# A planner's durations set anew, and TensorE's order of the same units searched again

## The chip, the cores and the metric

The kernel runs on one core of a Trainium2 chip, with its five engines: TensorE (PE), which multiplies matrices into PSUM; VectorE (DVE) and ScalarE (ACT), which read PSUM and write SBUF; GpSimd (POOL), which computes in SBUF and issues DMAs; and SyncE (SP), which issues DMAs. Each engine works through its own queue in the order written. The metric is the time of one execution on the device, in microseconds (us).

## The reference: what is computed

Talking-heads attention, and then a feed-forward layer with a squared ReLU. There are 8 batches, 12 heads, 448 positions, 64 columns in a head; the layer goes from 768 to 2048 and back.

```
scores = einsum('bhij,hg->bgij', q k^T / 8, w_pre)
attn   = softmax(scores)
attn   = einsum('bhij,hg->bgij', attn, w_post)
x      = attn v,  heads side by side: 3584 x 768
out    = relu(x w_in)^2 w_out
```

w_pre and w_post mix the twelve heads, the first before the softmax and the second behind it.

## The kernel before

The kernel is a set of *tasks*, each a short piece of work of one engine, and a *planner* (`_Plan`) that puts them in order when the program is built. All of it is decided then; on the chip each engine runs its list and waits on semaphores.

The tasks of one batch follow the data. "tr" units (L718) transpose q and k on PE; "tev" copies bring them to SBUF as `qkt`. "qk" units (L864) form scores for a tile of up to 128 rows, two heads at a time; twelve "sev" copies put the tile into `stage` (L478 on ACT, L479 on DVE). "rel" transfers, issued by SP (L910), lay the scores of 10 rows and 12 heads on 120 partitions of one slot of `dring`, which has 16 slots: the relayout. Then a "pre" unit (L933) mixes heads with `wk1` for two such slots, two "exp" tasks on ACT (L950) form the exponentials and their sums in `pring`, "rec" on DVE takes reciprocals, and "fold" and "tail" on POOL (L971, L986) multiply them into the weights `wk2s` and into `ptail`. A "post" unit (L1016, L1031) mixes heads again, and two "a2ev" copies bring the result to `a2t` (L478, L479). When half of a batch's rows are there, three "av" units (L1097) multiply by v and "xtev" copies give `xt`. The feed-forward layer has "h" units (F1; L1148 in batches 0 and 1, L1176 in the others), "relu" and "sq" tasks (L1204 or L1205, L1214), and "o" units (F2; L1293, the last two tiles L1242), each half of a unit pair of 16 matmuls; copies "oev" and transfers "odma" by POOL bring the output away. Batch 0 takes a shorter way for its first 22 slots: "dir" units (L815) with q scaled by the weights (products "sc", L793). Its weights `w_in_sb` and `w_out_sb` are loaded meanwhile. Before the first data "warm" matmuls (L591) run on a constant, and later in some gaps of the first 60 us; how many is worked out from the gap that the planner expects.

PE's units belong to ten streams (tr, qk, pre, post, av, dir, two of F1, two of F2), and the order within a stream is fixed. Which stream comes next is a digit of the string `ORDER`, one digit per unit: 948 of them. A program outside of the kernel searched for that string with the planner's costs. The planner (`run`, L306) takes PE's units in that order and places every other task by itself: of the tasks whose inputs it takes to be ready, the one that can start first; a copy or ReLU marked `FLEX` goes to ACT or DVE, whichever it expects to finish sooner. So the order on ACT, DVE, POOL and SP follows from the costs too.

```
streams = [[] for _ in range(10)]
s_T, s_QK, s_pre, s_post, s_AV, s_dir = streams[:6]
s_F1, s_F2 = streams[6:8], streams[8:]
...
per_engine, _ = plan.run(ORDER)
```

Each task has a cost per engine, `(held, lat)`: how long it occupies the engine, and after how long its result can be used. PE's costs are in `c_pe` and `unit`, the general ones of copies in `c_ev`. A change of the array's mode between units (row halves, quarters, column halves, full) costs `MODE_SWITCH`. Transfers are modelled as two kinds, "move" (relayouts) and "load" (the rest): a start (`DMA_START`, and up to `DMA_AHEAD` behind loads already on the way), work that slows while both kinds move (`dma_next`), and an end (`DMA_END`). `FETCH` (`fetch_wait`) prices PE's fetching of instructions, in blocks of 256. PSUM has eight banks; a unit takes the one or two that come free first, and waits for the copies that read them.

Of the kernel before, what the change touches and what calls it, by code (L numbers as in the profile page):

```python
# [10 lines left out]
PE = "pe"  # L11
# [7 lines left out]
MODE_SWITCH = 106.0  # L19
ACT_BIAS = 14.5  # L20
BLOCK = 256
FETCH = (110e3, 6000.0, 4600.0, 1400.0)
DMA_START = {"move": 1420.0, "load": 1350.0}
DMA_AHEAD = 3900.0
DMA_SLOW = {"move": 1.0, "load": 1.04}
DMA_END = {"move": 3700.0, "load": 2300.0}
INF = float("inf")
ORDER = (
    "0011055055105510551555511155555553115550013555555553135002555555335555335531002555112551"
    "1233332412423432266311771316622237673313676331677222444312767612267731367331671216767322"  # L30
    "2679339339221922833831020182244430026721810038111811181318322667133762227667331673337226"
    "2244433276113177300226761116722833833382128002672117667020367223833831181118122442293391"
    "3193119223932193139224422443393163116117200272263163723733632167022076211673372200833811"
    "1822289111933391139222244383183318113822244442236116317137116226373020273621363723722006"
    "2116733720209331913191192228183318331822224439319111933392224444222838316316338113822711"
    "7200263363722176313637212762002673317242020913191119133922244181338221831381383228224441"
    "3813633836702207622267117611633733762126733720018381228382200919111911393224422913931931"
    "3922283811383138322444422267161373611366222673173713736223673217392219812938338398222444"
    "22833873833867667672227676367678338444867676767676677679989998889899"
# [60 lines left out]
class _Plan:  # L100
# [97 lines left out]
    def dma_push(self, t, start):  # L198
# [3 lines left out]
        if kind == "move" and at < 30e3:  # L202
            at += 600.0
        elif kind == "move" and not self.moving["move"]:
            behind = sum(x[1] for x in self.moving["load"] if x[0] <= at)
            at += min(DMA_AHEAD, max(0.0, behind - max(0.0, at - self.moved)))
        self.moving[kind].append([at, work, packet, t])

    def dma_next(self, go=False):
# [7 lines left out]
        while True:  # L217
# [6 lines left out]
            if all(on):  # L224
                rate = (0.22, 0.52)
                if b[2] <= 200.0:
                    rate = (47.8 / (54.0 + b[2]), 0.72)
# [10 lines left out]
        if go:  # L238
            self.moved = now
            for i, y in enumerate((a, b)):  # L240
                if y is not None:
# [4 lines left out]
                        + (1800.0 if t.dma[0] == "load" and 20e3 < now < 45e3 else 0.0))  # L246
# [98 lines left out]
def bass_talking_heads_attention__then__ffn_squared_relu_kernel(  # L345
# [45 lines left out]
    with ExitStack() as es:  # L391
# [68 lines left out]
        def c_pe(t):  # L460
            return {PE: (t, t + 190.0)}
# [9 lines left out]
        def unit(s, name, fn, deps, ns, mode, group, mms):  # L471
            t = add(name, PE, fn, deps, c_pe(ns), 0, mode, group, 2 * mms)
# [156 lines left out]
        def load_v(b, u, h0, deps, after, prio):  # L629
            def fn(eng, en):  # L630
# [7 lines left out]
                            dma=("load", 870.0, 60.0))  # L638
# [63 lines left out]
        def emit_T(b):  # L702
            pb = b % 2
            for a in range(3):
                g = _Group(2)
                trs = []
                for i, src in enumerate((qraw, kraw)):
# [5 lines left out]
                    def fn_tr(eng, en, a=a, g=g, i=i, src=src, o0=o0):  # L713
                        r_ = None
                        for t in range(NT):
                            o = o0 + (POS[t] if i else t) * PJ
                            for u, c in QUADS:
# [9 lines left out]
                                7 * 32.0 + 18.0, "quad", g, 4 * NT)  # L727
# [20 lines left out]
                for u in range(2):  # L748
                    p = 3 * u + a

                    def fn_ev(eng, en, u=u, p=p, g=g):
# [3 lines left out]
                               {ACT: (820.0, 970.0), DVE: (545.0, 625.0)}, b * 1000.0 - 700)  # L755
# [91 lines left out]
        def emit_QK(b, T):  # L847
# [8 lines left out]
            for p in ((0, 3, 1, 4, 2, 5) if n == 0 else range(0, NP, IT // w)):  # L856
                g = _Group(2)

                def fn_qk(eng, en, p=p, g=g):
                    r_ = None  # L860
                    for x, y in QUADS:
                        if y * w < IT:
# [13 lines left out]
                            205.0 if quad else 190.0, "quad" if quad else "row", g,  # L876
                            4 if quad else 2)
                t_qk.after += old
                for x, y in QUADS:
# [3 lines left out]
                    def fn_sev(eng, en, x=x, y=y, p=p, g=g):  # L883
# [4 lines left out]
                                c_ev(S), b * 1000.0 + 20 + 10 * T)  # L888
# [14 lines left out]
        def emit_rel(b, c, n, r0, d0, nv):  # L903
# [4 lines left out]
            def fn(eng, en):  # L908
# [5 lines left out]
                         {SP: (850.0 if b == 0 else 1050.0, 0.0)}, g * 1.0, sem, 16,  # L914
# [10 lines left out]
        def emit_pre(g0):  # L925
# [3 lines left out]
            def fn_pre(eng, en):  # L929
                r_ = None  # L930
                for x, y in QUADS:
                    if x < len(gs):
# [7 lines left out]
                         205.0, "quad", gr, 2 * len(gs))  # L940
# [4 lines left out]
        def after_pre(g, t_pre, gr, x):  # L945
# [3 lines left out]
            def fn_exp(eng, en):  # L949
# [4 lines left out]
                        {ACT: (520.0, 645.0)}, b * 1000.0 - 900 + c)  # L954
# [8 lines left out]
            def fn_rec(eng, en):  # L963
# [3 lines left out]
                        {DVE: (82.0, 160.0)}, b * 1000.0 - 900 + c)  # L967

            def fn_fold(eng, en):
# [7 lines left out]
                         {POOL: (330.0, 370.0), DVE: (200.0, 280.0)},  # L977
# [7 lines left out]
            def fn_tail(eng, en):  # L985
# [6 lines left out]
                         {POOL: (340.0, 380.0), DVE: (200.0, 280.0)},  # L992
# [6 lines left out]
        def emit_post(g0):  # L999
# [10 lines left out]
            def fn_post(eng, en):  # L1010
# [12 lines left out]
                for x in range(2):  # L1023
# [5 lines left out]
                    else:  # L1029
# [8 lines left out]
                          nr * 28.0 + 2.0, "row", gr, 2 * nr)  # L1038
# [3 lines left out]
            for x in range(2):  # L1042
                def fn_a2(eng, en, x=x):
# [8 lines left out]
                           {ACT: c_ev(nr * PR * 1.16)[ACT], DVE: c_ev(nr * PR * 1.02)[DVE]},  # L1052
# [407 lines left out]
```

## Time and profile before

| | |
|---|---|
| time, median of 3 runs | 523.26 us |
| lowest and highest run | 522.7, 524.12 us |
| span of the profiled execution, first to last instruction | 522.5 us |
| time of the profiled execution | not listed apart; the span is 0.2 us under the lowest run and 0.76 under the median |
| mean granted clock of TensorE | 1.000 |
| PE, ACT, DVE, POOL busy | 508.7, 432.9, 402.8, 264.7 us |
| moved by DMA | 72.36 MB |

In a group's row come the line, the engine, the operation, what it writes and reads, the shapes and the count; behind the bar the busy time in us and the mean in ns of one, then the idle time of the engine ahead of these instructions and what ended most of it. "PEld" is the loading of weights, which runs beside the matmuls. The chain of waits follows the work that ended last, back from the end: a row has a start in us, a length in us and what ran. A matmul's shown end is modelled, and matmuls overlap, so in the chain a group lasts until the next group starts. "issue" is time in which an engine waited for nothing that the profile shows.

### The profile page before, as it was taken

The numbers are of one execution on the slowest core, as the hardware profiler recorded it, in microseconds if no ns is written. First come the engines' busy times: TensorE is split into PE (matmuls) and PEld (weight loads), VectorE is DVE, ScalarE is ACT, GpSimd is POOL, SyncE is SP. The second block draws the span as 40 slices with busy tenths as digits, with TensorE's granted clock in tenths as the row PEclk, the third lists the DMA queues.
The fourth block names the chain that finished last, engine by engine and source line by source line (L and its number), as shares of the span: only waits on it lengthen the run. The fifth ranks groups of instructions, "written<-read, shape, count | busy, mean of one in ns | idle before, by whom it ended". The sixth has DMA issues, their size and how long they took to land.

```text
span 522.5 us, 23103 instructions
## 1 busy us (share of the span) xinstructions
PE 508.7 (97%) x9477; PEld 320.4 (61%) x9477; DVE 402.8 (77%) x1038; ACT 432.9 (83%) x1243; POOL 264.7 (51%) x571
## 2 busy tenths in 40 slices
PE   8999999899989999999999999999999999999997
PEld 3455677567757665557546665566555665568874
DVE  8988878779969879977798868986797857955440
ACT  4899989889989889988998898999788899867421
POOL 9926556534753477335672486435654354243000
PEclk9999999999999999999999999999999999999999
DMA  8999989945995489646994689537985557451013
GB/s 113 194 228 181 215 166 182 191 93 114 170 192 131 108 163 180 146 94 155 177 183 86 138 174 191 125 70 159 175 141 114 132 129 136 85 128 53 3 24 99
DMA packets 83024, 72.36 MB, mean 138 GB/s; under 512 B 7160, under 2 KB 80424, under 8 KB 82920
## 3 DMA queue, kind: packets, MB, share of 16 engines
q0 software_dynamic: 37632, 33.83, 39.8%
q1 hardware_dynamic: 45000, 36.86, 29.2%
q8 instruction: 76, 1.25, 1.0%
q14 instruction: 28, 0.23, 0.1%
q10 hardware_dynamic: 288, 0.20, 0.1%
HBM read 47.27 MB, written 11.01 MB: 112 GB/s over the span
## 4 chain that ended last, share of the span: by engine, by line
PE 81%; DVE 7%; ACT 5%; DMA 5%; issue 1%; POOL 0%; SPq 0%; DVEq 0%
PE ps L1293 25%; PE ps L1176 18%; PE ps L933 6%; PE ps L1016 6%; PE ps L1097 6%; PE ps L864 5%; PE ps L815 5%; DMA dring<-stage 5%; PE ps L1148 4%; ACT pring L950 3%; DVE stage L479 2%; PE ps L1242 2%; PE ps L718 2%; PE ps L591 1%; DVE qkt L479 1%
## 5 line engine op out<-in xcount | busy, mean ns | idle before, releaser
L950 ACT ACTIVATE pring<-ps 128x448 bf16<-128x448 f32 x360 | 192.0, 560 | 12.9 <-PE ps L933 11.8
L1293 PE MATMUL ps<-w_out_sb,h2t 64*128 64x384 bf16 x1664 | 151.6, 323 | 2.3 <-issue 1.7
L971 POOL TENSOR_TENSOR wk2s<-wk2b,rinv 128x120 bf16<-128x120 bf16 (+1 forms) x179 | 70.5, 394 | 142.3 <-DVE rinv L964 141.2
L479 DVE CAST a2t<-ps 128x420 bf16<-128x420 f32 (+1 forms) x202 | 122.2, 640 | 15.5 <-PE ps L1031 14.4
L1176 PE MATMUL ps<-xt,w_in_sb 64*128 64x448 bf16 (+2 forms) x1344 | 120.7, 323 | 0.1
L478 ACT ACTIVATE stage<-ps 128x448 bf16<-128x448 f32 (+1 forms) x195 | 101.2, 556 | 14.9 <-PE ps L864 11.9
L478 ACT ACTIVATE a2t<-ps 128x420 bf16<-128x420 f32 (+1 forms) x166 | 99.7, 655 | 15.5 <-PE ps L1031 15.3
L479 DVE CAST stage<-ps 128x448 bf16<-128x448 f32 (+1 forms) x165 | 98.9, 615 | 16.8 <-PE ps L864 13.0
L1293 PEld LDWEIGHTS ps<-w_out_sb,h2t 64*128 64x128 bf16 x1664 | 77.5, 94 | 52.0 <-issue 4.0
L1176 PEld LDWEIGHTS ps<-xt,w_in_sb 64*128 64x128 bf16 x1344 | 61.7, 94 | 40.0 <-PE ps L933 2.0
L1325 POOL DMA_DIRECT2D out_dram<-osb x52 | 33.6, 652 | 100.8 <-ACT pring L950 39.6
L950 ACT ACTIVATION_READ_ACCUMULATOR pring<-ps 128x1 f32 x360 | 81.2, 226 | 0.0
L986 POOL TENSOR_TENSOR ptail<-pring,rinv 128x128 bf16<-128x128 bf16 x171 | 70.2, 411 | 0.0
L1016 PEld LDWEIGHTS ps<-wk2s,pring 60*128 60x128 bf16 x2160 | 47.7, 94 | 25.9 <-DVE stage L479 2.3
L1205 DVE TENSOR_SCALAR h1t<-ps 128x448 bf16<-128x448 f32 (+2 forms) x99 | 46.9, 482 | 14.4 <-PE ps L1176 11.3
L1016 PE MATMUL ps<-wk2s,pring 60*128 60x60 bf16 x2160 | 55.1, 187 | 2.3 <-DVE stage L479 1.1
L1214 DVE TENSOR_TENSOR h2t<-h1t 128x448 bf16<-128x448 bf16 (+2 forms) x176 | 55.5, 345 | 2.1 <-ACT h1t L1204 1.5
L933 PE MATMUL ps<-dring,wk 64*64 64x448 bf16 (+1 forms) x676 | 52.6, 363 | 1.4 <-ACT stage L478 0.8
L964 DVE RECIPROCAL rinv<-rowsum 128x2 f32<-128x2 f32 (+1 forms) x184 | 29.0, 157 | 31.5 <-ACT pring L950 30.7
L864 PE MATMUL ps<-qkt 64*128 64x448 bf16 (+1 forms) x360 | 50.3, 353 | 1.5 <-DVE stage L479 0.6
L1204 ACT ACTIVATE h1t<-ps 128x448 bf16<-128x448 f32 (+2 forms) x77 | 35.0, 461 | 14.4 <-PE ps L1176 12.6
L1097 PEld LDWEIGHTS ps<-a2t,vraw 128*64 128x64 bf16 x960 | 38.5, 109 | 6.0 <-ACT osb L478 2.4
(60 smaller groups left out, 536.8 us busy)
## 6 DMA issues: line engine op xcount, KB each, us to landing
dring<-stage SPq DMA_DIRECT2D x309, 105.0 KB
out_dram<-osb POOLq DMA_DIRECT2D x52, 192.0 KB, 3.9
vraw<-in_v_dram POOLq DMA_DIRECT2D x48, 128.0 KB
qraw<-in_q_dram POOLq DMA_DIRECT2D x48, 112.0 KB, 5.2
kraw<-in_k_dram POOLq DMA_DIRECT2D x48, 112.0 KB, 4.9
w_in_sb<-in_moe_w_in_dram POOLq DMA_DIRECT2D x8, 384.0 KB, 19.6
w_out_sb<-in_moe_w_out_dram POOLq DMA_DIRECT2D x8, 384.0 KB, 16.0
dring<-stage SPq DMA_DIRECT2D x30, 42.0 KB
```

Of the source, the lines that this page charges most:

```text
L478: return eng.activation(o, i_, AF.Copy)
L479: return eng.tensor_copy(o, i_)
L864: r_ = eng.matmul(ps[y * w:(y + 1) * w, g.banks[x], 0:S], qkt[r0:r0 + 64, pb, p + y, 0, i0:i0 + w], qkt[r0:r0 + 64, pb, p + y, 1, :], star ...
L933: r_ = eng.matmul(ps[64 * y:64 * y + 64, gr.banks[x], 0:S], wk1[64 * x:64 * x + 64 - R0 * x, :], dring[64 * x:64 * x + 64 - R0 * x, (g0 + ...
L950: return eng.activation(pring[:, pr, 0:S], ps[:, gr.banks[x], 0:S], AF.Exp, accum_out=rowsum[:, pr, :])
L971: return eng.tensor_tensor(wk2s[:, p0:p0 + n, :], i0.to_broadcast([128, n, PR]), rinv[:, p0:p0 + n, :].to_broadcast([128, n, PR]), ALU.mult)
L986: return eng.tensor_tensor(ptail[:, p0 // 2, :, :], pring[:, p0:p0 + 2, 0:PJ], rinv[:, p0:p0 + 2, :].to_broadcast([128, 2, PJ]), ALU.mult)
L1016: r_ = eng.matmul(ps[:, gr.banks[x], o0:o0 + PR], pring[64 * x:64 * x + PR, pr + y, (2 * k + 1) * PJ:(2 * k + 3) * PJ], wk2s[64 * x:64 * x ...
L1097: r_ = eng.matmul(po, vraw[:, h, sl, :], m, start=(k == 0), stop=(k == NS))
L1176: r_ = eng.matmul(ps[:, g.banks[x], 0:n], w_in_sb[64 * y:64 * y + 64, ft, t * 128:(t + 1) * 128], xt[64 * y:64 * y + 64, ft, c0:c1], start ...
L1214: return eng.tensor_tensor(h2t[:, t16, o0:o0 + n], h1t[:, s, 0:n], h1t[:, s, 0:n], ALU.mult)
L1293: r_ = eng.matmul(ps[:, g.banks[hh], 0:FH], h2t[64 * y:64 * y + 64, t16, col:col + 128], w_out_sb[64 * y:64 * y + 64, t16, hh * FH:(hh + 1 ...
```

## The change

The costs of the planner are set to other figures: of units on PE, of copies, exponentials and small products, of relayouts, loads and output transfers, of a change of mode and of instruction fetching. The rates at which a relayout and a load share the transfers' time, a formula before, come from a table by the size of the load's packets. The string `ORDER` is another, of the same length and with the same count of each digit. No task is added or taken away and none computes anything else. The first run of "warm" matmuls becomes 15 for 14, since the planner expects another gap there.

The whole diff follows, but for the rest of the two strings and for lines that stay.

```diff
-MODE_SWITCH = 106.0
+MODE_SWITCH = 97.0
...
-FETCH = (110e3, 6000.0, 4600.0, 1400.0)
-DMA_START = {"move": 1420.0, "load": 1350.0}
-DMA_AHEAD = 3900.0
+FETCH = (110e3, 4750.0, 3910.0, 1200.0)
+DMA_START = {"move": 1000.0, "load": 1270.0}
+DMA_AHEAD = 4400.0
...
-DMA_END = {"move": 3700.0, "load": 2300.0}
+DMA_END = {"move": 2950.0, "load": 2700.0}
+DMA_SHARE = {97.0: (0.295, 0.774), 79.0: (0.333, 0.747), 88.0: (0.363, 0.746),
+             60.0: (0.386, 0.842), 250.0: (0.496, 0.957), 54.0: (0.4, 0.75)}
...
 ORDER = (
-    "0011055055105510551555511155555553115550013555555553135002555555335555335531002555112551"
...
+    "0050115055105105511555555115555500315555511155555553335555533150025555335555020235511155"
...
-            at += 600.0
+            at += 1950.0
...
-                rate = (0.22, 0.52)
-                if b[2] <= 200.0:
-                    rate = (47.8 / (54.0 + b[2]), 0.72)
+                rate = DMA_SHARE[b[2]]
...
-                        + (1800.0 if t.dma[0] == "load" and 20e3 < now < 45e3 else 0.0))
+                        + (880.0 if t.dma[0] == "load" and 20e3 < now < 45e3 else 0.0))
...
-        def c_pe(t):
-            return {PE: (t, t + 190.0)}
+        def c_pe(t, mode=None):
+            return {PE: (t, t + (165.0 if mode == "quad" else 148.0))}
...
         def c_ev(cols):
...
         def unit(s, name, fn, deps, ns, mode, group, mms):
-            t = add(name, PE, fn, deps, c_pe(ns), 0, mode, group, 2 * mms)
+            t = add(name, PE, fn, deps, c_pe(ns, mode), 0, mode, group, 2 * mms)
...
             return plan.add("ldv%d_%d_%d" % (b, u, h0), POOL, fn, deps, {POOL: (610.0, 0.0)},
...
-                            dma=("load", 870.0, 60.0))
+                            dma=("load", 1160.0, 60.0))
...
                     t_tr = unit(s_T, "tr%d_%d_%d" % (b, a, i), fn_tr,
...
-                                7 * 32.0 + 18.0, "quad", g, 4 * NT)
+                                7 * 32.0 + 2.0, "quad", g, 4 * NT)
...
                     t_ev = add("tev%d_%d" % (b, p), FLEX, fn_ev, trs + [qk_done.get(b - 2)],
-                               {ACT: (820.0, 970.0), DVE: (545.0, 625.0)}, b * 1000.0 - 700)
+                               {ACT: (820.0, 970.0), DVE: (535.0, 607.0)}, b * 1000.0 - 700)
...
                 t_qk = unit(s_QK, "qk%d_%d_%d" % (b, T, p), fn_qk,
...
-                            205.0 if quad else 190.0, "quad" if quad else "row", g,
+                            200.0 if quad else 190.0, "quad" if quad else "row", g,
...
                     t_sev = add("sev%d_%d_%d_%d" % (b, T, p + y, x), FLEX, fn_sev, [t_qk] + old,
-                                c_ev(S), b * 1000.0 + 20 + 10 * T)
+                                {ACT: (423.0, 549.0), DVE: (545.0, 611.0)},
+                                b * 1000.0 + 20 + 10 * T)
...
             t = plan.add("rel%d_%d_%d" % (b, c, d0), SP, fn, sev_of[n] + [t_zero],
-                         {SP: (850.0 if b == 0 else 1050.0, 0.0)}, g * 1.0, sem, 16,
+                         {SP: (830.0, 0.0)}, g * 1.0, sem, 16,
...
             t_pre = unit(s_pre, "pre%d" % g0, fn_pre, rel[g0] + rel[g0 + 1] + [t_wk1],
-                         205.0, "quad", gr, 2 * len(gs))
+                         197.0, "quad", gr, 2 * len(gs))
...
             t_exp = add("exp%d_%d" % (b, c), ACT, fn_exp, [t_pre, t_init] + old_users(g),
-                        {ACT: (520.0, 645.0)}, b * 1000.0 - 900 + c)
+                        {ACT: (518.0, 635.0)}, b * 1000.0 - 900 + c)
...
             t_rec = add("rec%d_%d" % (b, c), DVE, fn_rec, [exp_of[g0], t_exp] + old_users(g),
-                        {DVE: (82.0, 160.0)}, b * 1000.0 - 900 + c)
+                        {DVE: (76.0, 176.0)}, b * 1000.0 - 900 + c)
...
             def fn_fold(eng, en):
...
             t_fold = add("fold%d_%d" % (b, c), DVE if g < 10 else POOL, fn_fold,
...
-                         {POOL: (330.0, 370.0), DVE: (200.0, 280.0)},
+                         {POOL: (347.0, 389.0), DVE: (195.0, 275.0)},
...
             t_tail = add("tail%d_%d" % (b, c), DVE if g < 10 else POOL, fn_tail,
...
-                         {POOL: (340.0, 380.0), DVE: (200.0, 280.0)},
+                         {POOL: (357.0, 403.0), DVE: (200.0, 280.0)},
...
             t_post = unit(s_post, "post%d" % g0, fn_post,
...
-                          nr * 28.0 + 2.0, "row", gr, 2 * nr)
+                          nr * 28.0 + 1.0, "row", gr, 2 * nr)
...
                 t_a2 = add("a2ev%d_%d" % (g0, x), FLEX, fn_a2, [t_post] + old,
-                           {ACT: c_ev(nr * PR * 1.16)[ACT], DVE: c_ev(nr * PR * 1.02)[DVE]},
+                           {ACT: (nr * PR * 0.967 + 85.0, nr * PR * 0.967 + 244.0),
+                            DVE: (nr * PR * 1.063 + 86.0, nr * PR * 1.063 + 189.0)},
...
                 t_av = unit(s_AV, "av%d_%d_%d" % (b, c0, p), fn_av,
...
-                            2 * ((7 * w + W1) / 2.4 + 5 * 2.9), "cols", g, 4 * (NS + 1))
+                            2 * ((7 * w + W1) / 2.4 + 5 * 2.4), "cols", g, 4 * (NS + 1))
...
                 def fn_x(eng, en, p=p, g=g, w=w):
...
                 t_h = unit(s_F, "h%d_%d_%d_%d" % (b, c0, t16, ph), fn_h,
...
-                           NFT * (n / 2.4 + 4.3), "row", g, 2 * NFT)
+                           NFT * (n / 2.4 + 2.5), "row", g, 2 * NFT)
...
             t_r = add("relu%d_%d_%d" % (b, c0, t16), FLEX, fn_relu, [t_h, h1_free.get(s)],
-                      c_ev(n), b * 1000.0 + 600)
+                      {ACT: (n / 1.2 + 61.0, n * 0.4 + 292.0),
+                       DVE: (n / 0.96 + 72.0, n * 0.526 + 266.0)}, b * 1000.0 + 600)
...
             t_s = add("sq%d_%d_%d" % (b, c0, t16), DVE, fn_sq,
...
-                      {DVE: (n / 1.92 + 80, n / 1.92 + 160)}, b * 1000.0 + 610)
+                      {DVE: (n / 1.92 + 70, n / 1.92 + 165)}, b * 1000.0 + 610)
...
-                               nk * (FH / 2.4 + 3.7), "full", g, nk)
+                               nk * (FH / 2.4 + 2.5), "full", g, nk)
                 def fn_oe(eng, en, hh=hh):
...
-                               nk * (FH / 2.4 + 3.7), "row", g, 2 * nk)
+                               nk * (FH / 2.4 + 2.5), "row", g, 2 * nk)
...
             t_od = plan.add("odma%d_%d" % (b, tile), POOL, fn_od, evs,
...
-                            sem_out[s], 32, dma=("load", 2200.0, 250.0))
+                            sem_out[s], 32, dma=("load", 1820.0, 250.0))
...
```

More of the change, by code (lines that the diff above doesn't have):

```diff
@@ L27 @@
 INF = float("inf")
 ORDER = (
-    "0011055055105510551555511155555553115550013555555553135002555555335555335531002555112551"
[L30 to L39, printed above, removed]
+    "0050115055105105511555555115555500315555511155555553335555533150025555335555020235511155"
@@ new lines @@
+    "1213332244433226763327613631222776133767131763137224442226766133677227673337631167267621"
+    "1913933292010938223812188320023342441326720018111811181338122666313771336722226677337622"
+    "2434413277313662020167613167221833833381228002672116737672007223811831183138122442291393"
+    "3931191322422931913392244224391633361711172020613622173736336217372200636212737020281381"
+    "1813182229393139311922243813831383118222444442236316337122761362020731711621362733720206"
+    "1126733720209139131913192228383318331822224419319113933192224442224831836316338311822007"
@@ L40 @@
+    "1172263363712276331637212762002617337202024419111911933392228181138131832283382238224444"
+    "1181163316720207631367222763367333762216733700228812283380201919111913391224422939131931"
+    "3922283813383118222444422376336173622267117361136371217621267337339228383912938839222444"
+    "22863863388733677672226766773673384448676767676767767689989989989988"
 )
```

## The prediction, made before the changed kernel ran

> **What bounds the kernel now.** I read the page first: busy shares, slices, chain, costliest groups.
>
> ```profile
> span 522.5 us, 23103 instructions
> PE 508.7 (97%) x9477; PEld 320.4 (61%) x9477; DVE 402.8 (77%) x1038; ACT 432.9 (83%) x1243; POOL 264.7 (51%) x571
> ...
> PE 81%; DVE 7%; ACT 5%; DMA 5%; issue 1%; POOL 0%; SPq 0%; DVEq 0%
> ...
> L1293 PE MATMUL ps<-w_out_sb,h2t 64*128 64x384 bf16 x1664 | 151.6, 323 | 2.3 <-issue 1.7
> L479 DVE CAST a2t<-ps 128x420 bf16<-128x420 f32 (+1 forms) x202 | 122.2, 640 | 15.5 <-PE ps L1031 14.4
> L478 ACT ACTIVATE a2t<-ps 128x420 bf16<-128x420 f32 (+1 forms) x166 | 99.7, 655 | 15.5 <-PE ps L1031 15.3
> ```
>
> TensorE (PE) is the bound: 97% busy and 81% of the chain. ACT at 83% and DVE at 77% empty PSUM behind it. Where PE still idles is told by the busy time of stages:
>
> ```profile
> 0.00:50.00 50.00, 46.69 (x725) 22.51 (x725) 43.13 (x108) 40.78 (x108) 34.37 (x68) 1.00 1.07 178
> 50.00:110.00 60.00, 56.27 (x1071) 41.01 (x1068) 48.09 (x142) 53.98 (x165) 34.70 (x76) 1.00 0.94 177
> 110.00:165.00 55.00, 52.92 (x1056) 37.70 (x1056) 47.84 (x141) 50.30 (x148) 29.93 (x66) 1.00 0.74 151
> 165.00:310.00 145.00, 144.24 (x2841) 87.43 (x2838) 118.84 (x290) 130.30 (x379) 79.82 (x176) 1.00 0.70 143
> 310.00:480.00 170.00, 169.64 (x3212) 102.37 (x3208) 131.73 (x312) 143.63 (x408) 81.47 (x178) 1.00 0.63 129
> 480.00:522.50 42.50, 38.96 (x590) 29.42 (x586) 13.21 (x49) 13.90 (x42) 4.38 (x9) 1.00 0.16 41
> ```
>
> After the stage's length come PE, weight load, DVE, ACT and POOL, then the granted clock (1.00 throughout). PE idles 3.3 us in the start, 3.7 in 50 to 110, 2.1 in 110 to 165, 0.8 and 0.4 in the long middle, and 3.5 in the last stage, whose end is copies and output after the last matmul. In 50 to 165 ACT is at 90 and 91%. So an order of PE's units has little to win after 165 us, and most of it between 50 and 165. The waits of PE, by what ended them:
>
> ```profile
> PE ps L1293 <- issue: 1.7, 1, 1.7
> PE ps L1016 <- DVE stage L479: 1.1, 2, 0.8
> PE ps L1016 <- POOL ptail L986: 0.8, 2, 0.5
> PE ps L933 <- ACT stage L478: 0.8, 1, 0.8
> PE ps L864 <- DVE stage L479: 0.6, 1, 0.6
> ```
>
> All waits ended by DVE, ACT or POOL outside the first warm-up come to 5.9 us in that view. They are understated, because a matmul's shown span runs on after the next could start. The chain of waits, which cuts spans at the next start, shows that:
>
> ```profile
> 355.38 1.30 PE ps L1293 x16
> ...
> 360.26 0.08 PE ps L1016 x6
> 360.34 0.03 PE ps L1031 x2
> 360.37 0.50 PE ps L933 x8
> ...
> 400.56 0.48 PE ps L718 x55
> 401.04 1.41 PE ps L1293 x16
> ```
>
> An F2 unit of 16 matmuls takes 1.30 us behind units of its own array mode and 1.41 behind a transpose of another mode: a change of mode costs about 0.10. Measured in this manner, from each unit's start to the next, over all 952 units (first 1.46 us, last 517.5), and less the usual length of the unit and 0.095 per change of mode, 69 units start more than 0.06 us late, together 15.9 us. Of it copies, exponentials, ReLUs and POOL's products end 10.5, the wait named "issue" 1.9, transfers and unclear ones 3.5. That is the pool from which the new order can win; the other 506 us are work that stays.
>
> **The change, part by part.** The same tasks run: 9478 matmuls for 9477, the same 376 transfers on SP in the same order (two of the last output pieces swap), the same POOL tasks with 178 of 541 places changed, weight loads at the same place among its products. Of some 1,000 copies and ReLUs eleven go from ACT to DVE and four the other way. So every effect lies in PE's order and what follows it.
>
> *Do the new figures match?* An F2 unit of 8 steps is planned with 8 x (160 + 2.5) = 1300 ns for 1310: the row has 1.30. The exponential is planned with 518 for 520, and four in a row start 0.517 apart:
>
> ```profile
> 301.55 0.54 ACT L950 ACTIVATE pring<-ps 128x448 bf16<-128x448 f32 x1
> ...
> 303.10 0.56 ACT L950 ACTIVATE pring<-ps 128x448 bf16<-128x448 f32 x1
> ```
>
> (three intervals in 1.55 us.) So the planner had PE 1% too slow; and copies of a2t it had at 471 (ACT) and 518 (DVE), now 491 and 532. It does what it says, and both errors pushed the old order the same way: too much eviction work behind PE.
>
> *Changes of mode*: 263 in the old order, 256 in the new, 7 x 0.10 = **-0.7 us**; nothing hides them.
>
> *Warm-up*: 15 matmuls for 14 ahead of the first transposes.
>
> ```profile
> 1.46 5.41 PE ps L591 x14
> ```
>
> 5.41 / 14 = **+0.4**. It is hidden if the first q tile comes later than 6.9 us, so the bounds are 0 and 0.4; I take 0.4, as PE ran matmuls right up to the transposes.
>
> *Late evictions*: For each 10 us of PE's own work (without waits) I added up the ACT and DVE time that its units set free, each copy at the spacing of back-to-back ones. Two engines do 20 us in that time. In the old order five stretches of 49 exceed it (the most 22.2), by 4.3 us together; in the new two (20.8), by 1.5: 65% less. With busy time per instruction from the groups instead (99.7/166 for an ACT a2t copy), the excess over 21 falls from 23.5 to 18.6, 21% less. I take a third of the 10.5 us, **-3.6**, nearer the second, since most waits are local and not from a full stretch; bounds 0 and -6.8.
>
> *Relayouts* (stage to dring, issued by SP, awaited by the pre units, L933). The planner now expects them sooner: start 1000 for 1420 ns and end 2950 for 3700, 1.2 us less, so it sets pre units closer behind them. The tightest that I found is pre240, third of three pre units, fed by the twelfth relayout of its tile:
>
> ```profile
> 286.13 0.37 PE L864 MATMUL ps<-qkt 64*128 64x448 bf16 x2
> ...
> 287.78 18.58 SPq L910 DMA_DIRECT2D dring<-stage  x18
> ...
> 305.06 0.76 PE L933 MATMUL ps<-dring,wk 64*64 64x448 bf16 x12
> ...
> kraw<-in_k_dram POOLq DMA_DIRECT2D x48, 112.0 KB, 4.9
> ...
> out_dram<-osb SPq DMA_DIRECT2D x6, 96.0 KB, 2.2
> ...
> 292.52 1.65 PE ps L1097 x40
> ```
>
> Issues are 18.58 / 18 = 1.03 us apart, so the twelfth leaves at 287.78 + 11 x 1.03 = 299.1; pre240 starts at 305.06 + 2 x 0.19 = 305.4, 6.3 later. No row has a relayout's landing; the transfer nearest in size takes 4.9 us, which leaves 1.4 us of room. The new order has one F2 unit (1.30), one AV unit (1.65/2) and three post units (0.2 each) less between, 2.7 us: a wait of 1.3. Likewise pre316 comes 4.2 us closer (13.7 to 9.4 us after the next to last QK unit of its tile): 1.65 + 3 x 1.03 + 4.9 = 9.6, a wait of 0.2. Six more come 0.4 to 6.8 us closer (pre72, pre100, pre208 to pre214) and I give them 0.5 together: before pre208 to pre214 much of the distance was spent while SP still issued for the tile ahead. In all **+2.0**. A late pre unit holds everything behind it in PE's queue, and ACT's exponentials with it; these waits are what comes next where an eviction wait goes. Ends: 0, with the 2.2 us of an SP output piece as landing, and +7, with 1.3 us over the 4.9 at four places. POOL's loads share these transfers' time (DMA share 0.6 to 1.07 in the stages), and no load moves by more than a few places.
>
> *Instruction blocks*: PE stands still 1.74 us at 149.7 with no engine to blame.
>
> ```profile
> q8 instruction: 76, 1.25, 1.0%
> ...
> 151.43 0.34 PE L1293 MATMUL ps<-w_out_sb,h2t 64*128 64x384 bf16 x2 [1.74 <-issue]
> ```
>
> 76 packets of 16 KB feed PE's instructions, 256 of them each, and the wait lies on such a border. Blocks that PE's own work passes within 5.6 us: 9 in the old order, one of which waited, 11 in the new, three of them in a row in the same stage. So one wait stays, **0**; bounds -1.7 and +3.4. [...]
>
> **Sum**: -0.7 + 0.4 - 3.6 + 2.0 + 0 = -1.9 us. The profiled span becomes 520.6; the median of the runs, 523.26, stands 0.76 above the span and becomes **521.4**.
>
> **Rivals.**
> *Half the gain* (0.22): evictions wait elsewhere instead, since both orders need the same copies and ACT stays at 90% in 50 to 165. With -1.8 in place of -3.6: 523.2, no change. For it: the 21% above. Against: the fullest stretch shrinks either way.
> *Relayouts decide* (0.31): slower. At four places (pre72, pre208 and its followers, pre240, pre316) the room is used up, so each us of landing beyond 4.9 costs four. At 1.3 us more it is 5.2: 526.6. From 0.9 us on it is slower by over 0.3%. For it: the chain spends 10.25 and 13.37 us on a relayout where loads run beside.
>
> ```profile
> 48.59 10.25 DMA dring<-stage
> 63.61 13.37 DMA dring<-stage
> ```
>
> Against: pre units had rooms of a us or more in most batches. [...]
> *No instruction wait* (0.10, within the forecast's chance): 1.7 less, 519.7.
>
> **Numbers.** Forecast 0.47, half the gain 0.22, relayouts 0.31. A measurement here tells about 0.3% (1.6 us). All bounds on one side give 514.1 and, with evictions at 0, 533.4; both are unlikely, and 517 to 527.5 leaves out about 2 in 10. The forecast's own range is 517 to 521.7. Faster 0.47, within 0.3% 0.22, slower 0.31.
>
> **What would show it.** Evictions: PE idle in 50 to 110 falls under 3 us. Relayouts: pre240, again third of three pre units and now ahead of the last AV unit of batch 4, starts about a us behind the second, with no engine's work ending its wait. Instruction blocks: one "issue" wait of over a us. Modes: 0.10 each as before. The prediction is wrong if PE idle in 165 to 480 grows beyond 3 us, or if that in 50 to 165 does not fall.

## The result, and the profile after

The changed kernel takes 530.5 us in the median (529.04 to 533.23, four runs), before 523.69 beside it (522.7 to 524.94): 1.0137 times as long, with an interval of 1.0095 to 1.0179. It is slower by 7 us, where 521.4 with a range of 517 to 527.5 was forecast. The profiled execution has a span of 527.3 us and a time of 529.04; it is the fastest of the four, so its profile shows 4.8 us of the loss. Medians and ratios from here on leave out executions more than 1.5% above the fastest of their kernel.

The page of the changed kernel, the lines that answer to those of before:

```profile
span 527.3 us, 23120 instructions
PE 509.6 (97%) x9478; PEld 321.3 (61%) x9478; DVE 403.2 (76%) x1047; ACT 429.8 (82%) x1234; POOL 265.7 (50%) x571
PE 77%; DMA 6%; DVE 6%; ACT 5%; SPq 2%; POOL 2%; issue 1%; DVEq 0%; ACTq 0%; POOLq 0%
```

Busy times hardly differ from before's. So the time is lost in gaps, and the chain says whose: PE fell from 81 to 77% of it, and SP's queue, at 0% before, has 2. Busy time by stage of the changed kernel, with the columns of before's table (length, PE, weight load, DVE, ACT, POOL, clock):

```profile
0.00:50.00 50.00, 46.66 (x718) 22.09 (x718) 43.66 (x110) 40.38 (x107) 35.67 (x69) 1.00 1.08 181
50.00:110.00 60.00, 59.29 (x1188) 43.96 (x1186) 50.60 (x147) 56.30 (x175) 36.58 (x80) 1.00 0.98 186
110.00:165.00 55.00, 53.85 (x1038) 38.45 (x1036) 48.07 (x140) 49.95 (x149) 29.50 (x65) 1.00 0.72 144
165.00:310.00 145.00, 138.39 (x2706) 84.35 (x2698) 113.74 (x283) 124.08 (x359) 75.42 (x166) 0.99 0.68 138
310.00:480.00 170.00, 167.70 (x3156) 98.86 (x3154) 130.47 (x313) 143.10 (x402) 82.93 (x182) 1.00 0.64 130
480.00:527.30 47.30, 43.75 (x702) 33.59 (x698) 16.71 (x57) 16.02 (x47) 5.59 (x11) 1.00 0.17 43
```

PE's idle time from 50 to 165 us fell from 5.8 to 1.9 us, as forecast. From 165 to 480 it rose from 1.1 to 8.9. Start and end are as before. Idle time is thus 3.9 us more; the other 0.9 of the 4.8 between the two spans is PE's own busy time, which got longer (the clock, below, adds 1.1 on one unit).

The waits of before and then of the changed kernel for relayouts (engine, line, what it waited for; us in total, times, longest):

```profile
DVE stage L479 <- DMA dring<-stage: 2.2, 2, 1.2
ACT stage L478 <- DMA dring<-stage: 2.0, 2, 1.0
```

```profile
DVE stage L479 <- DMA dring<-stage: 7.9, 5, 2.9
...
PE ps L1178 <- DVE rinv L965: 4.0, 2, 2.8
ACT stage L478 <- DMA dring<-stage: 3.6, 4, 1.3
...
PE ps L934 <- DMA dring<-stage: 2.0, 2, 1.1
```

So 4.2 us of waits on relayouts became 13.5, and most are not where the prediction looked, at PE's pre units: they are at the copies that *write* `stage`. `stage` holds two tiles. A copy of tile n must wait until every relayout that reads tile n-2 has landed, and while it waits DVE stands still in its own queue, with reciprocals and copies behind it for which PE waits. The timeline of the changed kernel shows the largest case:

```profile
199.69 10.17 SPq L911 DMA_DIRECT2D dring<-stage  x10
...
202.38 0.54 ACT L478 ACTIVATE stage<-ps 64x448 bf16<-64x448 f32 x1 [0.89 <-DMA dring<-stage]
202.48 0.62 DVE L479 CAST stage<-ps 64x448 bf16<-64x448 f32 x1 [2.93 <-DMA dring<-stage]
203.02 0.15 DVE L965 RECIPROCAL rinv<-rowsum 128x2 f32<-128x2 f32 x1
...
204.63 2.42 PE L1178 MATMUL ps<-xt,w_in_sb 64*128 64x448 bf16 x12 [2.78 <-DVE rinv L965]
...
207.42 1.31 PE L1178 MATMUL ps<-xt,w_in_sb 64*128 64x448 bf16 x12
```

DVE stands 2.93 us, PE 2.78 after it. Then the same twelve matmuls take 2.42 us in place of 1.31. The granted clock (the number behind POOL's) says why, in three stretches of the changed kernel:

```profile
200.00:203.80 3.80, 1.84 (x44) 1.09 (x40) 1.29 (x3) 2.91 (x8) 0.80 (x3) 1.00 1.04 178
203.80:207.30 3.50, 2.67 (x32) 1.52 (x34) 2.75 (x7) 0.11 (x1) 2.11 (x5) 0.51 0.77 161
207.30:212.00 4.70, 4.70 (x83) 2.29 (x78) 4.50 (x11) 4.33 (x11) 1.27 (x3) 1.00 0.67 149
```

For 3.5 us, the last 0.8 of the gap of 2.78 us among them, TensorE ran at 0.51 of its clock; the stretches before and behind have 1.00.

The other route, a pre unit that waits for its own slices, is also there, and pre240 has it as forecast (timeline, then chain, of the changed kernel):

```profile
305.85 0.57 PE L934 MATMUL ps<-dring,wk 64*64 64x448 bf16 x8
307.55 0.38 PE L934 MATMUL ps<-dring,wk 64*64 64x448 bf16 x4 [1.13 <-DMA dring<-stage]
```

```profile
303.24 4.22 DMA dring<-stage
```

Two pre units run, the third starts 1.7 us after the first of them and 1.13 late; 1.3 was worked out. A single relayout landed 4.2 us after its issue, where 4.9 was taken.

### The profile page after: what moved, and what is told of

Read it like the earlier page. It is cut to its first block, busy times and chain, and to the rows that moved or that the text cites. A ratio compares the mean times of both kernels' runs of the same rounds, so it can differ in the third digit from the quotient of the medians.

```text
span 527.3 us, 23120 instructions
## 1 busy us (share of the span) xinstructions
PE 509.6 (97%) x9478; PEld 321.3 (61%) x9478; DVE 403.2 (76%) x1047; ACT 429.8 (82%) x1234; POOL 265.7 (50%) x571
## 4 chain that ended last, share of the span: by engine, by line
PE 77%; DMA 6%; DVE 6%; ACT 5%; SPq 2%; POOL 2%; issue 1%; DVEq 0%; ACTq 0%; POOLq 0%
PE ps L1296 21%; PE ps L1178 18%; PE ps L934 6%; PE ps L1099 6%; PE ps L1150 6%; DMA dring<-stage 6%; PE ps L1017 5%; PE ps L864 5%; PE ps L815 5%; ACT pring L951 3%; DVE stage L479 3%; SPq L911 2%; PE ps L1245 2%; PE ps L718 2%; DVE a2t L479 1%
## 5 line engine op out<-in xcount | busy, mean ns | idle before, releaser
L479 DVE CAST a2t<-ps 128x420 bf16<-128x420 f32 (+1 forms) x207 | 123.5, 636 | 20.1 <-PE ps L1032 18.9
L1178 PE MATMUL ps<-xt,w_in_sb 64*128 64x448 bf16 (+2 forms) x1344 | 122.4, 325 | 4.1 <-DVE rinv L965 4.0
L478 ACT ACTIVATE stage<-ps 128x448 bf16<-128x448 f32 (+1 forms) x198 | 102.6, 552 | 17.4 <-PE ps L864 13.1
L478 ACT ACTIVATE a2t<-ps 128x420 bf16<-128x420 f32 (+1 forms) x161 | 96.9, 653 | 18.2 <-PE ps L1032 17.7
L479 DVE CAST stage<-ps 128x448 bf16<-128x448 f32 (+1 forms) x162 | 96.9, 615 | 18.2 <-PE ps L864 9.2
L951 ACT ACTIVATION_READ_ACCUMULATOR pring<-ps 128x1 f32 x360 | 79.7, 221 | 0.0
L1207 DVE TENSOR_SCALAR h1t<-ps 128x448 bf16<-128x448 f32 (+2 forms) x103 | 49.4, 484 | 16.7 <-PE ps L1178 13.7
L1217 DVE TENSOR_TENSOR h2t<-h1t 128x448 bf16<-128x448 bf16 (+2 forms) x176 | 52.8, 331 | 1.5 <-ACT h1t L1206 0.9
L864 PE MATMUL ps<-qkt 64*128 64x448 bf16 (+1 forms) x360 | 51.6, 354 | 1.2 <-DVE qkt L479 0.6
L1206 ACT ACTIVATE h1t<-ps 128x448 bf16<-128x448 f32 (+2 forms) x73 | 32.8, 456 | 14.8 <-PE ps L1178 13.7
```

Source lines behind the costliest of these rows:

```text
L478: return eng.activation(o, i_, AF.Copy)
L479: return eng.tensor_copy(o, i_)
L864: r_ = eng.matmul(ps[y * w:(y + 1) * w, g.banks[x], 0:S], qkt[r0:r0 + 64, pb, p + y, 0, i0:i0 + w], qkt[r0:r0 + 64, pb, p + y, 1, :], star ...
L951: return eng.activation(pring[:, pr, 0:S], ps[:, gr.banks[x], 0:S], AF.Exp, accum_out=rowsum[:, pr, :])
L1178: r_ = eng.matmul(ps[:, g.banks[x], 0:n], w_in_sb[64 * y:64 * y + 64, ft, t * 128:(t + 1) * 128], xt[64 * y:64 * y + 64, ft, c0:c1], start ...
L1217: return eng.tensor_tensor(h2t[:, t16, o0:o0 + n], h1t[:, s, 0:n], h1t[:, s, 0:n], ALU.mult)
```

## The experiments

R stands throughout for the theory that the relayouts land later than the new figures say, so that the order asks for them too early; P for the theory that the placement or the order loses in another way. Before's median in the groups of runs was 522.7 to 523.2 us. What a planner expects of a span is called its plan.

**Costs and order apart.** `e1_costs` is after with before's `ORDER`; `e2_order` is before with after's `ORDER`.

```diff
 ORDER = (
-    "0050115055105105511555555115555500315555511155555553335555533150025555335555020235511155"
+    "0011055055105510511555511155555113555550013555555553135002555555335555335531002555112551"
```

> The new costs with the old string ORDER. Theory R (the new order of TensorE sets pre and QK units closer behind relayouts than these land, at the pre units themselves and at the copies into stage, which hold up DVE and ACT): PE's order is the old one, so 521 to 525 us, and DVE, ACT and PE together wait about 4 us for dring transfers, as before. Rival P (the new costs make the planner place work on ACT, DVE, POOL and SP badly, whatever PE's order): 528 us or more.

> The old costs with the new string ORDER. Theory R: PE's order keeps its short distances, so 528 to 535 us, and the waits for dring transfers stay at 10 us or more. Rival P: placement is the old one, so back to about 524 us.

Measured: `e1_costs` 526.34 us, 1.0063 (1.0031 to 1.0094); `e2_order` 531.29, 1.0166 (1.0104 to 1.0228). So the order carries the loss: it is slow even under the old costs. The new costs alone, through the other engines' order, cost about 3 us, 1.3 beyond the range that R gave and short of P's; the waits on relayouts of `e1_costs` are 2.0 us, less than before's, and no other row of its one profile explains these 3. They stay unexplained.

**The two routes closed by hand.** In after's `ORDER` digit 1 is a QK unit and 2 a pre unit. `e4_qk` puts later the seven QK units whose copies had waited at `stage`; `e5_pre` puts four pre units later. One row of the string from each:

```diff
-    "2434413277313662020167613167221833833381228002672116737672007223811831183138122442291393"
+    "2434413277313662020167613167221833833382281002672116737672007223881131183138122442291393"
```

```diff
-    "2434413277313662020167613167221833833381228002672116737672007223811831183138122442291393"
+    "2434413277313662020167613167218233833381228002672116737672007223811831183138122442291393"
```

> The changed kernel with seven QK units at five places moved 1.3 to 3.8 us later in ORDER (qk2_3_0, qk3_0_0, qk3_0_1, qk3_3_0, qk4_3_0, qk7_1_0, qk7_1_1), so that their copies find the old contents of stage already moved. Theory R: DVE's wait for dring transfers falls from 7.9 to under 3.5 us and the time by 3 to 5 us, to 525.5 to 527.5. Rival (only the pre units' own waits cost time, the copies' waits are hidden): 529.5 to 531.

> The changed kernel with four pre units moved 1.5 to 2.3 us later in ORDER (pre110, pre188, pre240, pre338, which waited 1.0, 1.0, 1.3 and 1.8 us). Theory R: these waits go, 3 to 5 us less, 525.5 to 527.5. Rival (each wait is taken up by the next unit in the queue, so the distance of the pre units decides nothing): 529.5 to 531.

Measured: 530.21 us (1.0136, 1.0082 to 1.0189) and 529.83 (1.0122, 1.0075 to 1.017): nothing clear of noise is won by either, and both times lie in the ranges of the rivals, not of R. The waits of `e4_qk`, then of `e5_pre`:

```profile
PE ps L934 <- DMA dring<-stage: 2.1, 1, 2.1
ACT stage L478 <- DMA dring<-stage: 1.6, 2, 1.4
```

```profile
DVE stage L479 <- DMA dring<-stage: 9.0, 4, 3.4
...
PE ps L1178 <- DVE rinv L965: 5.4, 2, 3.2
ACT stage L478 <- DMA dring<-stage: 4.2, 3, 1.9
```

`e4_qk` brought DVE's row at `stage` from 7.9 us to 0.4 and left a longer pre wait; `e5_pre` emptied PE's row at the pre units and left more at `stage`. In the profile of `e4_qk`, its fastest execution with a span of 526.3 us, these rows come to 4.1 us, no more than before's 4.2; so they don't show all that the order loses. With both moves (`e6_both`), and with after's order under the longer relayout costs (`e3_relcosts`):

> After, with both moves at once: seven QK units later (as in e4_qk) and four pre units later (as in e5_pre), costs untouched. R (two routes of one cause, which stand in for each other when only one is closed): waits of VectorE and ScalarE at stage under 4 us together and of TensorE on dring under 2 us, TensorE's idle time in 165-485 down from 8.9 to some 4 or 5: 525 to 527. If each route only moves the wait on to a later tile, as each alone did: 529 to 532.

> After's order, with the relayouts' three figures put back in the planner: TensorE's work is the same, only the other engines' and queues' placement (who copies, when slices are asked for) is chosen by the longer figures. R: the slices land when they land, so the order decides: 528 to 531, slower than before, with 8 us or more of waits on dring. P (the order is sound, and the shorter figures only placed the copies badly): 522 to 525.

```diff
 # e3_relcosts, against after
-DMA_START = {"move": 1000.0, "load": 1270.0}
+DMA_START = {"move": 1420.0, "load": 1270.0}
...
-DMA_END = {"move": 2950.0, "load": 2700.0}
+DMA_END = {"move": 3700.0, "load": 2700.0}
...
-                         {SP: (830.0, 0.0)}, g * 1.0, sem, 16,
+                         {SP: (850.0 if b == 0 else 1050.0, 0.0)}, g * 1.0, sem, 16,
```

Measured: `e6_both` 526.9 (1.0061, 1.0025 to 1.0096): about half of the loss is gone, as R had it in time, though in its profile the copies still wait 5.4 us at `stage` (R: under 4) and PE idles 6.3 from 165 to 485 (R: 4 or 5). `e3_relcosts` 533.1 (1.016, 1.0097 to 1.0222), 2.1 above R's range: the old prices no longer help, since TensorE's order is fixed.

**The search done again.** Four orders, each searched anew from before's order in the same time and manner, with the relayouts' figures as the only difference; then two more, in which the search weighed beside the put-back figures a second, still later landing (`e7_searched`, and `e12_longer`, from the order of `e7_searched` and four times as long). For `e7_searched` the expectation doesn't say so; that of `e9_both_back`, its clean form, does.

> After's costs untouched, and ORDER searched anew under them from before's order, as long as for the kernel with the relayouts' figures put back: the same search, other relayout costs. R: the search again puts tiles closer to their use than they land, as it did for after's order: waits on dring of 8 us or more in all, a median of 527 to 534, slower than before, though its own plan is shorter than that of the kernel with the figures put back. P or 'after's order is one unlucky draw of the search': 518 to 523, like the other searched order.

> All three figures of a relayout put back (SP held 1050, start 1420, end 3700), ORDER searched anew under that one set of costs, for the same time and from the same start as in e8_control (in e7_searched the search had weighed a second, still later landing beside it, so it was no clean counterpart of e8_control). R (the relayouts' figures make the difference): 521 to 526, waits on dring of 4 us or less, against 538.1 of e8_control. If the second, later landing in the search of e7_searched made the difference: 530 or more.

> Only the time SP is held by a relayout put back (830 to 1050), start and end as in after; ORDER searched anew under that, as long. It tells which figure misled. Under the full set put back, this order's plan is 517.4 us long, 3.9 longer than that of e9_both_back: if SP's figure is the larger part (a tile of 13 relayouts comes some 2.9 us later by it, against 1.2 us by start and end together): 524 to 528. If start and end are: 530 or more.

> Only start (1420) and end (3700) put back, SP held 830 as in after; ORDER searched anew, as long. Under the full set put back this order's plan is 523.4 us long. If SP's figure is the larger part: 529 to 534, near after. If start and end are: 522 to 526.

> After's costs with the three figures of a relayout put back to before's (start 1420, end 3700, SP held 1050 each but 850 in the first eight units), and ORDER searched anew under these costs. R (the relayouts' figures are what misled the search; all the other new costs are sound): the tiles stand where the DMA can deliver them, so the waits on dring stay at before's level (VectorE and ScalarE at stage 4 us or less together, TensorE at the pre units 1 us or less), TensorE's idle time in 165-485 is under 3 us, and the eviction gain in 50-165 is kept: a span of 516 to 520, a median of 517 to 521, faster than before. P (a new order as such is slow, whatever the relayouts cost: gaps from what no cost holds, such as instruction blocks and the clock): 526 or more, as with after's order.

> As e7_searched (all three put back, a second, later landing weighed beside them in the search), searched four times as long, from e7_searched's order. Its plan is 1.1 us shorter than e7_searched's (512.6 against 513.8). R: 520.5 to 523, faster than before by 0 to 2 us. If what the plan does not hold (the small waits by which e7_searched's trace falls 7.8 us behind its plan, spread evenly) decides at this level: 522 to 525, no change.

The edits are those of the diff above (all three lines for `e9_both_back`, `e7_searched` and `e12_longer`, the last alone for `e10_sp_back`, the first two for `e11_land_back`, none for `e8_control`) and another `ORDER`.

| kernel | relayout figures | plan, us | waits on relayouts in the profile, us | median, us | ratio, interval |
|---|---|---|---|---|---|
| before (all costs old) | old | 522.7 | 4.2 | 522.8 | |
| after | new | 509.6 | 13.5 | 530.5 | 1.0137 (1.0095 to 1.0179) |
| e8_control | new | 512.5 | 23.5 | 538.14 | 1.0267 (1.022 to 1.0314) |
| e11_land_back | start, end old | 512.4 | 8.8 | 530.92 | 1.0135 (1.008 to 1.019) |
| e10_sp_back | SP's time old | 511.8 | 11.8 | 528.53 | 1.0101 (1.0052 to 1.0149) |
| e9_both_back | all three old | 513.5 | 2.8 | 526.54 | 1.008 (1.0045 to 1.0116) |
| e12_longer | and later still | 512.6 | 6.3 | 524.4 | 1.0023 (0.9989 to 1.0056) |
| e7_searched | and later still | 513.8 | 1.2 | 523.6 | 0.9996 (0.9966 to 1.0027) |

The plans of all new orders are within 4.2 us of each other, and their times 14.5 apart. (A ratio is to before's runs on the same chip; the 522.8 is one such median. The waits, those of weight loads among them, are of one execution each and sort the times only roughly.) What sorts the times is how late the search believed the slices to land: 538.1 with the new figures, 526.5 with the old. By the ranges set beforehand SP's time is the larger part, but how much each brings isn't shown: each has one search, and the two orders made under the new figures, after's and `e8_control`'s, are 7.6 us apart.

The planner itself could have told. Given the put-back figures and after's other costs, it plans before's order at 519.0 us, after's at 524.5 and that of `e8_control` at 529.5, against 513.5 for `e9_both_back`: the two orders made under the new figures are then the longest, as on the chip. The waits of `e8_control`, and then of `e7_searched`:

```profile
DVE stage L479 <- DMA dring<-stage: 8.0, 4, 3.5
...
PE ps L934 <- DMA dring<-stage: 6.6, 2, 3.6
ACT stage L478 <- DMA dring<-stage: 4.9, 3, 3.2
...
PEld ps L934 <- DMA dring<-stage: 4.0, 1, 4.0
```

```profile
DVE stage L479 <- DMA dring<-stage: 0.9, 1, 0.9
...
ACT stage L478 <- DMA dring<-stage: 0.3, 1, 0.3
```

`e8_control` ended 4.1 us above R's range, `e9_both_back` and `e10_sp_back` 0.5 us each above the ranges that they came nearest to, and neither `e7_searched` nor `e12_longer` beat before, as R had said they would. So no kernel here is faster than before with the work whole.

**Early landings under an unchanged order.** The search experiments change the order with the figures. The last four leave the order alone and let the slices land earlier: half of each relayout's rows are left out from the third batch on, in after, before, `e8_control` and `e9_both_back`.

```diff
+                m = nv if b < 2 else max(1, nv // 2)
-                eng.dma_start(dring[o:o + nv * H, slot, :],
-                              stage[r0:r0 + nv, n % 2, :, :]).then_inc(sem.handle, 16)
+                eng.dma_start(dring[o:o + m * H, slot, :],
+                              stage[r0:r0 + m, n % 2, :, :]).then_inc(sem.handle, 16)
```

> After with half of every relayout left out from the third batch on: each moves half of its rows, so part of the scores in the ring is stale and the output is not the reference's; TensorE, the copies, ORDER and every wait are untouched. So the relayouts land early without a change of the order. R (the slices land later than the order asks for them, and nothing else ails it): the waits on dring go, the even drift of the other searched orders stays: 517 to 522, below the same cut made in before. P (after's order loses its time in other ways too): 525 or more.

> Before with the same half of every relayout left out. Its order waits 4.2 us on dring at the copies, and its TensorE idles under 1 us in 165 to 480: 520 to 523, within 0.5% of before under R and P alike. After with that cut, less this, is what the new order is worth where the relayouts cannot hold it: by the terms of the prediction without the relayouts', 3 to 4 us in the new order's favour.

> The order of e8_control (538.1 us, waits of 23 us on dring) with the same half of every relayout left out. R: 518 to 524, near the other searched orders, a fall of 14 us or more. P: 530 or more.

> The order of e9_both_back (526.9 us, one wait of 2.8 us on dring at 377 us) with the same half of every relayout left out. If its 4 us over before are a last tile or two that still come late: 519 to 523. If they are its own (the even drift behind the plan): 525 to 528.

| order of | whole, us | half, us | fall |
|---|---|---|---|
| after | 530.5 | 520.22 | 10.3 |
| before | 523.19 | 521.11 | 2.1 |
| e8_control | 538.14 | 523.41 | 14.7 |
| e9_both_back | 526.54 | 521.73 | 4.8 |

The ratios to before with whole relayouts are 0.9948 (0.9924 to 0.9973) for after's order and 0.9967 (0.9946 to 0.9989) for before's. After's order loses nothing more once its slices come early, while before's, with the same rows left out, gains 2.1 us; so the late slices are the cause of its loss, and of that of `e8_control` and of the 4 us of `e9_both_back` too. The semaphores in the traces tell how early: from the first issue of a tile to the landing of its last slice (mean of the 21 tiles issued after 150 us) after takes 15.9 us and `e13_after_half` 14.0, and after's planner had expected 13.8. The half relayouts thus give the order the landings that it was made for. The same place as above in `e13_after_half`, DVE and then PE:

```profile
202.16 0.62 DVE L479 CAST stage<-ps 64x448 bf16<-64x448 f32 x1 [1.22 <-DMA dring<-stage]
```

```profile
204.30 1.31 PE L1179 MATMUL ps<-xt,w_in_sb 64*128 64x448 bf16 x12 [1.07 <-ACT a2t L478]
```

DVE waits 1.22 us in place of 2.93, PE 1.07 in place of 2.78, and the unit takes 1.31 again. All four times lie in the ranges set for late slices. Leaving the rows out also takes transfers away from beside the loads (104 GB/s move from 165 to 310 us, for 138), which these runs can't part from the relayouts' own time.

## Why the prediction was wrong, point by point

- **The figures match, "it does what it says"** (the step that failed). Two of PE's and ACT's figures were compared with rows, the relayouts' were not. Of their change the prediction counts start and end, 1.2 us, and leaves out SP's time, though the row stood in it: 18.58 us for 18 issues, 1.03 each, where the new cost says 0.83 (the changed kernel: 10.17 for 10). Over a tile of 13 relayouts the last is issued 12 x 0.19 = 2.3 us later than planned. The traces agree: from a tile's first issue to its last, after's planner expected 9.2 us and 11.4 passed (the 21 tiles above), and this is the whole of the 2.2 us by which its last slice is late. The search had taken up room that isn't there. 0.83 is near the usual issue; the mean is higher, since some take much longer (of the changed kernel, shortest/median/longest in ns):

```profile
L911 SPq DMA_DIRECT2D dring<-stage x367: 673/807/2516, 17.7 to 474.3; - x184
```

- **Start and end** were no error of the new costs: from issue to landing a relayout issued from 165 to 480 us takes 4.8 us in the mean in after (2.5 to 8.8), and its planner expected 4.8. Under the old costs before's planner expected 6.4 where 4.7 passed; by this a tile that was planned with 17.9 us landed in 15.6, and late slices had room. `e10_sp_back` has SP's time right and this room gone: its tiles take 16.1 us, as planned, and yet it waits 11.8 us on relayouts. A figure that is right in the mean leaves an order without room for the slices that come later than the mean.
- **Relayouts, +2.0** (the term of the sum that was too small). Missing was the second user of the same transfers, the copies that reuse `stage`: DVE's and ACT's waits there grew by 7.3 us (4.2 to 11.5), where the prediction has no term. PE's idle time from 165 to 480 rose by 7.8 us, against +2.0, beyond the upper end of 7. At the pre units pre240 came as worked out, 1.13 for 1.3. That PE's row there reads 2.0, the forecast, is luck: its other wait is that of pre188 (0.87), which wasn't named, while pre72, pre100, pre208 to pre214 and pre316, which were, didn't wait for slices. The rival "relayouts decide" had sign and cause, 526.6 at 0.31, but only the four pre units as its places.
- **The clock** had no term: 0.51 of it for 3.5 us around the end of one gap, 1.1 us on one unit.
- **Late evictions, -3.6.** Right in place and sign: start to start, over 0.06 us late, and without waits behind a late relayout, they fell from 10.5 to 8.0 us, -2.5.
- **Instruction blocks, 0.** The 1.74 us wait is gone and the largest "issue" wait left on PE is 0.3, -1.4, within the bounds. The order needn't be why: `e1_costs`, with before's order, has no such wait either. That such waits are gone for good can't be concluded: `e2_order` has two, the longest 3.3, both on a border of 256 instructions as the planner counts them:

```profile
PE ps L1176 <- issue: 3.8, 2, 3.3
```

- **Modes, -0.7, and warm-up, +0.4**: too small to be seen; the first stage is busy 46.66 us for 46.69.
- **From span to median.** An execution takes 1.7 us more than its span (529.04 and 527.3). So before's profiled execution took some 524.2, above its median. Part of the waits that it showed may have belonged to that execution: before's order with half relayouts idles 0.3 us from 110 to 165, where 2.1 stood, though the relayouts are shorter there too.

```profile
110.00:165.00 55.00, 54.66 (x1116) 39.19 (x1114) 49.81 (x145) 51.83 (x150) 31.31 (x69) 1.00 0.60 114
```

Of the 3 to 4 us that the order was to be worth without the relayouts, 520.22 against 521.11 leaves 0.9, and the two intervals overlap. That the pool, read from one execution, was too large for the typical one would explain it; no run shows that.

Of what was to show it: idle from 50 to 110 under 3 us came (0.7), pre240 too, one "issue" wait of over a us didn't; the idle time from 165 to 480 beyond 3 us, named as what would make it wrong, did.

## What to carry to other kernels

When a planner's durations change, compare each with the trace, first of all those of transfers: a search turns every optimistic figure into an order that relies on it, so a better plan can be a slower kernel. Where durations scatter, a median is such a figure, and even the mean leaves no room. Plan an order found under new figures with the old ones too: where they differ by several us, the order hangs on the figures. For a buffer that a transfer reads, list both who waits for the data and who waits for the room; the second may be a copy that blocks an engine's whole queue. An order that leaves room for late transfers cost little here (`e7_searched`: 0.9996), and in the largest case a late slice cost PE a gap of 2.78 us and 1.1 more by the clock.

## What was not expected of the hardware

- From the timelines and, last, a stretch of the busy time: TensorE ran at 0.51 of its clock for 3.5 us around the end of an idle time of 2.78 us, from 2.0 us into it on; behind gaps of 1.13 and 1.07 us its matmuls took their usual time (0.38 us for four, 1.31 for twelve). In `e9_both_back` slow matmuls followed 2.75 us as well: 24 of them, 2.6 us at 1.31 for twelve, take 3.69, and the clock of 374 to 381 us is 0.76 in the mean. One gap of 2.97 us in `e8_control` was not followed by it (the clock of the next 3.4 us is 1.00), so in these runs the length of a gap alone doesn't tell what the clock does.

```profile
377.38 0.59 PE L934 MATMUL ps<-dring,wk 64*64 64x448 bf16 x4 [2.75 <-DMA dring<-stage]
377.90 3.69 PE L1178 MATMUL ps<-xt,w_in_sb 64*128 64x448 bf16 x24
```

```profile
311.65 0.38 PE L934 MATMUL ps<-dring,wk 64*64 64x448 bf16 x4 [2.97 <-DMA dring<-stage]
```

```profile
311.60:315.00 3.40, 3.35 (x67) 2.12 (x69) 1.32 (x3) 1.32 (x5) 2.54 (x6) 1.00 1.01 164
```

- SP issues relayouts of 105 KB one per 1.02 to 1.03 us in the two stretches read (10.17 us for 10 in after, 18.58 for 18 in before), and half of all its issues in after take under 0.81 us. In after's 21 tiles the issues take 11.4 us of the 15.9 from the first issue to the last landing; a single landing takes 4.8 us in the mean.
